# A transformer block on one Trainium2 core: an order written by a list scheduler, five-bank exp groups, and attention on four 32-wide strips

## The chip, the cores and the metric

The kernel runs on one core of a Trainium2 chip. The core's engines work side by side and meet only through semaphores: TensorE (PE) multiplies matrices and writes PSUM, VectorE (DVE) and ScalarE (ACT) compute element by element, GpSimd (POOL) does small things on SBUF, SyncE (SP) issues transfers. Each engine takes its instructions strictly in the order in which they stand in its program. The metric is the device time of one execution in microseconds (us). A profile of one further execution is at hand.

## The reference

One token sequence of 2048 rows of 640 passes through an adaLN-conditioned attention and a gated bilinear feed-forward; all tensors are bf16.

```python
mod = (_silu(c) @ w_mod)                      # six vectors of 640: sa, ca, ga, sb, cb, gb
h = _layernorm(x) * (1 + ca) + sa
q, k, v = split(h @ wqkv)                     # 32 heads of 20
p = softmax(q @ k.T * 20 ** -0.5)             # 2048 x 2048 for each head
x = x + ga * ((p @ v) @ wo)
h = _layernorm(x) * (1 + cb) + sb
x = x + gb * (((h @ w_gate) * (h @ w_up)) @ w_down)    # 640 -> 1536 -> 640
```

## The kernel before

**Layout.** Queries go in four chunks of 512; for each chunk and each group of heads the scores are computed transposed, with 128 keys on the partitions and 512 queries along the row. A *block* is one such 128x512 score tile of one head: 32 heads x 16 key tiles x 4 chunks = 2048 blocks. K and Q lie in tiles of four heads, each head padded to 32 rows (`KT_sb`, `QT_sb`), so that a score matmul has 32 rows and up to four of them can stand on different row strips of the array. V has 24 columns a head, the first of them 1, so that the row sums of the softmax fall out of the same matmul.

**A step.** Heads are taken in sets of three (`SETS`, eleven sets, the last with two). A step is one set and one key tile: three score matmuls (L1130) into one of two triples of PSUM banks, one exp by ACT over the triple (L1146, 128x1536 into a ring `Pbuf` of four), three PV matmuls (L1159) that accumulate into bank 6 on three column strips. There are 4 x 11 x 16 = 704 steps. After the 16 steps of a set, DVE transposes the result (L1183), takes the reciprocal of the row sums (L1187), multiplies (L1189) and transposes back (L1193) into `Oc`, in which each set has a row block of its own.

**What sets the order.** The order is a loop over steps: exp of step g, scores of step g+2, PV of step g, then `xs.inject(g)`. That call puts other matmuls, *X work*, into the gap, a bounded number of nanoseconds for each step, from a list of tasks whose accumulations all go to bank 7: first the projections that were not done before the loop, then, once a chunk of attention is finished, its *suffix*: out-projection (L959, eleven matmuls a round, one for each set), residual add (L968), LayerNorm (L980 to L988), the multiply and add with the modulation vectors (L990, L992), transposes (L999) and their eviction (L1005), gate (L1036), its eviction (L1041), up (L1049), the product (L1054), down (L1073), the last add (L1083), the store. w_down is scaled by the vector gb on DVE in every chunk (L934). A step with nothing to put in gets a filler matmul of 32 rows (L852). The suffix of the fourth chunk comes after the last exp, with all eight banks.

**The head.** Before the loop: POOL clears the padded weight tiles (L512 to L515) and then issues the load of wqkv (L561); ACT takes square roots (L583) and the sigmoid (L653); PE makes all six modulation vectors, broadcast over the partitions (L663); ACT copies the weights into padded tiles (L690 to L698); each of the four token tiles is normalised (L568 to L592), transposed (L615), evicted by ACT with shift and scale (L620), and gets the first half of V (L746, L752) and the first K and Q tiles (L724, L734). ACT then zeroes two row blocks of `Oc` (L861, L868).

## Time and profile before

| | us |
|---|---|
| time, median of three runs (lowest to highest) | 1135.11 (1135.11 to 1136.35) |
| span of the profiled execution, first to last instruction | 1138.6 |
| busy: PE, ACT, DVE, POOL | 952.1, 969.7, 390.4, 37.8 |
| first exp starts, last exp starts | 91.4, 1059.8 |
| mean granted PE clock | 0.913 |

The profiled execution has no time of its own beside its span; the span lies 3.5 us above the median of the runs. A row of a group in the profile reads: line, engine, operation, out<-in with shapes, count, then the busy time of the group and the mean duration of one in ns, then the idle time of the engine ahead of it and who ended it. A row of the order of time reads: start, length, engine, line, and in brackets the idle time before it. A row of windows reads: the window, its length, busy us of each engine with instruction counts, the granted clock as a share of full speed, the share of the DMA engines and GB/s.

### The profile page before, as it was taken

To read this page: it belongs to the slowest core of one execution; us is meant where nothing else is said; L and a number is where in the kernel's file an instruction comes from. 1 tells how busy PE (TensorE), PEld (TensorE's weight loads), DVE (VectorE), ACT (ScalarE), POOL (GpSimd) and SP (SyncE) were. 2 spreads that over 40 slices of the span, in tenths; PEclk is the share of its full clock that TensorE was granted. 3 is DMA by queue.
4 is the path that set the end of the run, shared out by engine and by line. 5 is a ranking of instruction groups with operands and counts; after the bars stand their busy time and mean duration, and the time that the engine had idled before them with its cause. 6 is when DMAs were issued, how large, how long until landed. Compare 5 with 4: busy or idle time off the path is not lost.

```text
span 1138.6 us, 14720 instructions
## 1 busy us (share of the span) xinstructions
PE 952.1 (84%) x6035; PEld 293.7 (26%) x6095; DVE 390.4 (34%) x690; ACT 969.7 (85%) x752; POOL 37.8 (3%) x52
## 2 busy tenths in 40 slices
PE   1677898899998888888997898889987888889778
PEld 0331222222222222222322222223222222223434
DVE  2741322344323333332114333321123333322475
ACT  1559999999999899999999999999987999999200
POOL 7000000000000000000000000000000000000000
PEclk9788999999989889898989779999977899989889
DMA  8100001000022001100230011100400011100422
GB/s 295 57 1 1 1 1 30 1 1 1 1 75 53 1 12 45 37 13 6 68 78 1 1 30 41 35 1 18 133 1 1 12 36 35 24 6 20 126 64 64
DMA packets 80418, 40.59 MB, mean 36 GB/s; under 512 B 64544, under 2 KB 80032, under 8 KB 80352
## 3 DMA queue, kind: packets, MB, share of 16 engines
q1 hardware_dynamic: 77328, 32.29, 11.0%
q10 hardware_dynamic: 2624, 4.92, 1.2%
q0 software_dynamic: 400, 2.46, 0.6%
q8 instruction: 48, 0.79, 0.3%
q14 instruction: 18, 0.15, 0.0%
HBM read 37.03 MB, written 2.62 MB: 35 GB/s over the span
## 4 chain that ended last, share of the span: by engine, by line
PE 39%; ACT 29%; issue 16%; DVE 13%; POOL 2%; another core or an unknown queue 0%; ACTq 0%; POOLq 0%
ACT Pbuf L1146 26%; PE ps_all L1159 9%; PE ps_all L1130 9%; PE ps_all L724 7%; PE ps_all L959 3%; PE ps_all L1036 3%; PE ps_all L1073 3%; PE ps_all L1049 2%; PE ps_all L746 2%; DVE OT L1183 2%; DVE KT_sb L734 1%; DVE QT_sb L734 1%; ACT hT L620 1%; PE ps_all L852 1%; DVE xn L990 1%
## 5 line engine op out<-in xcount | busy, mean ns | idle before, releaser
L1146 ACT ACTIVATE Pbuf<-ps_all 128x1536 bf16<-128x1536 f32 (+1 forms) x704 | 928.9, 1526 | 40.6 <-PE ps_all L1130 39.4
L1130 PE MATMUL ps_all<-QT_sb,KT_sb 32*128 32x512 bf16 x2048 | 296.1, 412 | 73.1 <-ACT Pbuf L1146 49.5
L1159 PE MATMUL ps_all<-Pbuf,V_sb 128*24 128x512 bf16 x2048 | 294.1, 412 | 9.0 <-DVE OT L1183 8.8
L1130 PEld LDWEIGHTS ps_all<-QT_sb,KT_sb 32*128 32x128 bf16 x2048 | 68.9, 92 | 323.7 <-ACT Pbuf L1146 244.2
L1159 PEld LDWEIGHTS ps_all<-Pbuf,V_sb 128*24 128x24 bf16 x2048 | 67.2, 89 | 189.4 <-issue 169.0
L959 PE MATMUL ps_all<-wo_sb,Oc 128*128 128x320 bf16 x352 | 76.7, 344 | 13.9 <-DVE h2T L1005 11.7
L1036 PE MATMUL ps_all<-h2T,wgst 128*128 128x512 bf16 x216 | 71.9, 410 | 9.8 <-DVE hprod L1054 4.4
L1073 PE MATMUL ps_all<-wd_sb,hprod 128*128 128x320 bf16 x384 | 72.5, 313 | 6.2 <-DVE wd_sb L934 5.4
L1049 PE MATMUL ps_all<-h2T,wust 128*128 128x512 bf16 x228 | 71.8, 398 | 4.9 <-DVE gsb L1041 3.4
L1183 DVE STREAM_TRANSPOSE OT<-ps_all 96x512 f32<-96x512 f32 (+1 forms) x44 | 31.3, 711 | 118.3 <-PE ps_all L1159 118.3
L1041 DVE COPY gsb<-ps_all 128x512 f32<-128x512 f32 x48 | 32.9, 685 | 89.8 <-PE ps_all L1036 82.4
L1054 DVE TENSOR_TENSOR hprod<-ps_all,gsb 128x512 bf16<-128x512 f32 x48 | 32.8, 684 | 89.9 <-PE ps_all L1049 78.8
L968 DVE TENSOR_TENSOR xck<-ps_all,xck 128x320 bf16<-128x320 f32 x32 | 15.3, 486 | 121.5 <-PE ps_all L959 121.5
L746 PE MATMUL ps_all<-Wv,hT 128*128 128x384 bf16 x160 | 40.6, 394 | 12.9 <-ACT hT L620 12.9
L1083 DVE TENSOR_TENSOR xck<-ps_all,xck 128x320 bf16<-128x320 f32 x32 | 15.5, 484 | 98.5 <-PE ps_all L1073 98.5
L724 PE MATMUL ps_all<-hT,Wk 128*128 128x512 bf16 x147 | 43.5, 394 | 6.3 <-DVE KT_sb L734 2.9
L724 PE MATMUL ps_all<-hT,Wq 128*128 128x512 bf16 x149 | 42.8, 383 | 5.3 <-issue 1.0
L734 DVE CAST KT_sb<-ps_all 128x512 bf16<-128x512 f32 x32 | 22.1, 691 | 67.1 <-PE ps_all L724 67.1
L959 PEld LDWEIGHTS ps_all<-wo_sb,Oc 128*128 128x128 bf16 x352 | 29.2, 106 | 51.8 <-issue 22.7
L734 DVE CAST QT_sb<-ps_all 128x512 bf16<-128x512 f32 x32 | 22.1, 692 | 56.0 <-PE ps_all L724 53.9
L1073 PEld LDWEIGHTS ps_all<-wd_sb,hprod 128*128 128x128 bf16 x384 | 30.3, 99 | 38.4 <-issue 17.9
L934 DVE TENSOR_TENSOR wd_sb<-wd_sb,mods_b 128x640 bf16<-128x640 bf16 x48 | 39.0, 813 | 0.0
(68 smaller groups left out, 433.5 us busy)
## 6 DMA issues: line engine op xcount, KB each, us to landing
wd_sb<-in_B_w_down_dram SPq DMA_DIRECT2D x4, 1920.0 KB, 9.4
wgst<-in_B_w_gate_dram SPq DMA_DIRECT2D x48, 160.0 KB, 2.7
wust<-in_B_w_up_dram SPq DMA_DIRECT2D x48, 160.0 KB, 2.8
wmod_sb<-in_w_mod_dram ACTq DMA_DIRECT2D x4, 1200.0 KB, 13.9
x<-in_A_x_dram SPq DMA_DIRECT2D x4, 640.0 KB, 7.1
xck<-in_A_x_dram SPq DMA_DIRECT2D x4, 640.0 KB, 4.3
out_dram<-xck SPq DMA_DIRECT2D x16, 160.0 KB, 1.8
wraw<-in_A_wqkv_dram POOLq DMA_DIRECT2D x5, 480.0 KB, 5.9
```

The lines of the kernel that those rows point to most:

```text
L724: fn = lambda e, b, kt=kt: e.matmul(psbank(b), Wx[:, kt, sg, :], hT[:, tc, kt, :], start=(kt == 0), stop=(kt == KT - 1))
L734: eve = dve.ins(lambda e: e.tensor_copy(dst[:, sg, tc * 512:(tc + 1) * 512], psbank(b)), inc=c_ev, waits=w)
L746: fn = lambda e, b, kt=kt: e.matmul(psbank(b)[:, 0:ncol], hT[:, tc, kt, (t % 4) * 128:(t % 4 + 1) * 128], Wv[:, kt, cc * ncol:(cc + 1) * n ...
L934: ev_wdp_l[0] = dve.ins(lambda e: e.tensor_tensor(wd_sb[:, fc, :], wd_sb[:, fc, :], mods_b[:, 2, :], ALU.mult), inc=c_ev, waits=[ev_wdl])
L959: fn = lambda e, b, j=j, tl=tl, nch=nch: e.matmul(ps_all[:, b, 0:320], Ocq[:, j, tl * 128:(tl + 1) * 128], wo_sb[:, j, nch * 320:(nch + 1) ...
L1036: fn = lambda e, b, kt=kt, stg=stg: e.matmul(psbank(b), wgst[:, stg, kt, :], h2T[:, kt, :], start=(kt == 0), stop=(kt == KT - 1))
L1049: fn = lambda e, b, kt=kt, stg=stg: e.matmul(psbank(b), wust[:, stg, kt, :], h2T[:, kt, :], start=(kt == 0), stop=(kt == KT - 1))
L1073: fn = lambda e, b, fc=fc, tl=tl, nch=nch: e.matmul(ps_all[:, b, 0:320], hprod[:, fc, tl * 128:(tl + 1) * 128], wd_sb[:, fc, nch * 320:(nc ...
L1130: fn = lambda e, bs=bs, i=i, sg=sg, s=s, cq=cq, kt=kt: e.matmul(ps_all[:, bs * 3 + i, :], KT_sb[32 * s:32 * s + 32, sg, kt * 128:(kt + 1) ...
L1146: fn = lambda e, sl=sl, nh=nh, bs=bs: e.activation(Pbuf[:, sl, 0:nh * 512], ps_sflat[bs][:, 0:nh * 512], ACT.Exp, scale=SCALE)
L1159: fn = lambda e, i=i, h=h, sl=sl, kt=kt: e.matmul(ps_all[32 * i:32 * i + VW, BO, :], V_sb[:, kt, h * VW:(h + 1) * VW], Pbuf[:, sl, i * 512 ...
L1183: ev_t1 = dve.ins(lambda e, rows=rows: e.transpose(OT[0:rows, :], ps_all[0:rows, BO, :]), inc=c_at, waits=[ev_pv[g], st["onorm"]] + extra)
```

## The change

The file is written anew. Arithmetic and results are the same, apart from where scalings are applied. What it does:

**The order comes from a list scheduler.** Every instruction is a task with a duration from a small table (for PSUM reads by DVE `ps_cost`, for SBUF `sb_cost`, 216 ns for a 512-column matmul, ACT `n/1.2 + 52`), dependencies, a priority and, for X work, a gate. A simulated clock advances while the kernel is being built; whenever an engine of the model is free it takes the ready task with the best priority, and the sequence that results is the program. PE takes, in this order: the next score group if its banks are free; PV if at least six blocks wait (or a ring runs low, or the set ends); X work; a filler. A filler is now a full 128-row matmul on 512 columns (L1475), put in whenever the modelled activity of the last 3.4 us is under a bound; there are 240, where there were 83. The gate of X work is a number of exp groups, spread evenly over the chunk that follows.

**Groups.** Heads are taken in eight sets of four, and the blocks of all sets follow each other in one list, which is cut alternately into groups of three (banks 0 to 2, ring `PA`) and of two (banks 3 and 4, ring `PB`): 410 exps of 1536 and 409 of 1024 columns (L944). X work gets banks 5 and 6, PV bank 7 on four column strips. V has 21 columns a head without padding; a PV matmul takes 32 columns, of which the last eleven belong to the next head and are not used.

**Head.** `x` and two of the six modulation vectors are loaded first; those two are computed as columns (25 one-column matmuls each, L626), the rest later. The rsqrt goes to POOL. Scores of item 0 (the first set) start when the first token tile is projected; the other three tiles follow while exps run.

**Ends of sets.** The four DVE steps stay (L1050 to L1058), on 128 rows. The second transpose writes `OcT`, from which 36 small SBUF-to-SBUF transfers per chunk put the heads into rows without gaps (L1069), so that an out-projection round has five matmuls (L1119), not eleven.

**Suffix.** The modulation is folded into the eviction after the transposes (L1156). POOL scales wo and w_down once (L858, L863). After the last exp the evictions of the gate are ACT's (L1199), and the gate and up weights of nine of the twelve column tiles are by then in the space of used-up queries. The code also holds a path that makes exps on DVE from shifted copies; `QUADS` is zero, so no such instruction is built.

In the rows below, `hT` is the normalised input transposed, `Wk`/`Wq`/`Wv` the projection weights, `KT`/`QT` the projected K and Q, `scol` the vector silu(c), `wm` parts of w_mod.

The start of PE's program before, up to the first scores (L1130):

```order
L663 MATMUL ps_all<-wmod_sb_84,SC_68 128x320 x60
L615 MATMUL ps_all<-ident_49,xn_10_58 128x128 x20
L746 MATMUL ps_all<-Wv_56,hT_54 128x384 x20
L724 MATMUL ps_all<-hT_54,Wk_55 128x512 x5
L724 MATMUL ps_all<-hT_54,Wq_90 128x512 x5
L615 MATMUL ps_all<-ident_49,xn_10_58 128x128 x20
L746 MATMUL ps_all<-Wv_56,hT_54 128x384 x20
L724 MATMUL ps_all<-hT_54,Wk_55 128x512 x5
```

(two more tiles follow in the same way), and now:

```order
L626 MATMUL ps_all<-scol_55,wm_20_68 128x1 x25
L626 MATMUL ps_all<-scol_55,wm_21_69 128x1 x25
L689 MATMUL ps_all<-ident_49,xn_87 128x128 x20
L738 MATMUL ps_all<-hT_88,Wk_89 128x512 x5
L738 MATMUL ps_all<-hT_88,Wq_90 128x512 x5
L770 MATMUL ps_all<-wV_91,hT_88 128x320 x5
L919 MATMUL ps_all<-QT_70,KT_67 128x512 x5
L770 MATMUL ps_all<-wV_91,hT_88 128x320 x10
L919 MATMUL ps_all<-QT_70,KT_67 128x512 x3
```

The first scores (L919) stand behind one token tile, not four. On ACT, what stands ahead of the first exp (L944) is now:

```order
L577 ACTIVATE ex_52<-csb_51 128x5
L718 COPY Wq_90<-wkq_82 128x5x4x20
L722 COPY Wq_90<-wkq_82 128x28x20 x5
L718 COPY Wk_89<-wkq_82 128x5x4x20
L722 COPY Wk_89<-wkq_82 128x28x20 x2
L696 ACTIVATE hT_88<-ps_all,mcol_56 128x512
L722 COPY Wk_89<-wkq_82 128x28x20 x2
L696 ACTIVATE hT_88<-ps_all,mcol_56 128x512
L722 COPY Wk_89<-wkq_82 128x28x20
L944 ACTIVATE PA_78<-ps_all 128x1536
```

Two of the five hT evictions of the first tile wait behind weight copies there. In the middle of the stream, during gate and up work, PE's program before is

```order
L1130 MATMUL ps_all<-QT_sb_86,KT_sb_85 128x512 x3
L1159 MATMUL ps_all<-Pbuf_78,V_sb_88 24x512 x3
L1049 MATMUL ps_all<-h2T_75,wust_94 128x512 x2
L1130 MATMUL ps_all<-QT_sb_86,KT_sb_85 128x512 x3
L1159 MATMUL ps_all<-Pbuf_78,V_sb_88 24x512 x3
L1049 MATMUL ps_all<-h2T_75,wust_94 128x512
```

and now

```order
L919 MATMUL ps_all<-QT_71,KT_67 128x512 x3
L1307 MATMUL ps_all<-PA_78,Vf_77 32x512 x3
L1307 MATMUL ps_all<-PB_79,Vf_77 21x512
L1307 MATMUL ps_all<-PB_79,Vf_77 32x512
L1307 MATMUL ps_all<-PA_78,Vf_77 32x512 x2
L1307 MATMUL ps_all<-PA_78,Vf_77 21x512
L919 MATMUL ps_all<-QT_71,KT_67 128x512 x2
L1191 MATMUL ps_all<-h2T_94,stg_97 128x512 x3
L919 MATMUL ps_all<-QT_71,KT_67 128x512 x5
```

PV stands in batches of seven or eight blocks behind every third score group, and X work in between. After the last exp PE had

```order
L959 MATMUL ps_all<-wo_sb_89,Oc_35_83 128x320 x44
L999 MATMUL ps_all<-ident_49,xn_22_70 128x128 x5
L959 MATMUL ps_all<-wo_sb_89,Oc_35_83 128x320 x22
L999 MATMUL ps_all<-ident_49,xn_22_70 128x128 x5
L959 MATMUL ps_all<-wo_sb_89,Oc_35_83 128x320 x22
L999 MATMUL ps_all<-ident_49,xn_22_70 128x128 x10
L1036 MATMUL ps_all<-h2T_75,wgst_93 128x512 x5
```

and now has

```order
L1475 MATMUL ps_all<-KT_67,ident_49 128x512 x12
L1119 MATMUL ps_all<-wo_98,Ocp_86 128x320 x40
L1475 MATMUL ps_all<-KT_67,ident_49 128x512 x6
L1151 MATMUL ps_all<-ident_49,xn_48_96 128x128 x20
L1475 MATMUL ps_all<-KT_67,ident_49 128x512
L1191 MATMUL ps_all<-h2T_94,stx_103 128x512 x10
```

All 40 out-projection matmuls stand together, and the transposes come after the fourth tile's LayerNorm. The diff, cut to the places that matter:

```diff
-    for g in range(min(lead, NSTEP)):
-        issue_scores(g)
-    for g in range(NSTEP):
-        P.cur_step = g
-        issue_exp(g)
-        if g + lead < NSTEP:
-            issue_scores(g + lead)
-        issue_pv(g)
-        ...
-        xs.inject(g)
...
-    SETS = [tuple(range(i, min(i + 3, H))) for i in range(0, H, 3)]
...
+SEM = 60.0
+PE_DRAIN = 170.0
+PE_SWITCH = 100.0
+ACT_LAT = 190.0
+DVE_LAT = 40.0
+DMA_RATE = 260.0
+HAM_W = 3413.3
+HAM_MIN = 2550.0
...
+CHUNKS = [(0, 512), (512, 512), (1024, 512), (1536, 512)]
+QUADS = [0, 0, 0, 0]
+def ps_cost(n):
+    return n * 1.042 + 110.0
+def sb_cost(n, rate):
+    return n * rate + 62.0
...
+    load_x(0, "sp", 1)
+    load_wm(0, wm_a[0], "act", 0)
+    load_wm(1, wm_a[1], "act", 1)
+    d_wK = load_w(1, "sp", 2, wkq[:, :, D:2 * D])
+    d_wQ = load_w(0, "act", 2, wkq[:, :, 0:D])
+    d_wV = load_w(2, "act", 3, wV[:, :, :])
+    load_x(1, "sp", 3)
+    load_x(2, "sp", 4)
+    load_x(3, "sp", 5)
...
+    GA = [0, 1, 2]
+    GB = [3, 4]
+    G = Slots([5, 6], "G")
+    BPV = 7
...
+    while ubuf:
+        k = 3 if gi_ % 2 == 0 else 2
+        glist.append(ubuf[:k])
+        ubuf = ubuf[k:]
+        gi_ += 1
...
+        ta = Task("act", nu * 512 / 1.2 + 52.0, fexp, [ts], prio=g, name=f"E{g}")
+        ta.acq = [(pool_, "p", nu)]
...
+        mc = VW if (4 * u.j + s) % 16 == 15 else 32
+        ...
+            ems.append(lambda e, i=i, kt=kt, stt=stt, stp=stp: e.matmul(
+                ps[32 * s:32 * s + mc, BPV, 0:u.n],
+                Vf[:, (kt * H + 4 * u.j + s) * VW:(kt * H + 4 * u.j + s) * VW + mc],
+                srcf()[:, i * u.n:(i + 1) * u.n], tile_position=(0, 32 * s), start=stt, stop=stp,
+                skip_group_check=True))
...
+    def pick_pe(t):
+        sc.pull("pe")
+        if pvstate["sidx"] < NG:
+            ts, us = score_q[pvstate["sidx"]]
+            if acquire_ready(ts, t):
+                start = mode_start("S", t)
+                dur, used = issue_S(ts, us, t, start)
+        ...
+        cands = pv_candidates(t, 10)
+        it = st_pv["item"]
+        if cands:
+            info = item_info[it]
+            nwork = sum(1 if k == "a" else 4 for k, _ in cands)
+            ring_low = min(len(pA.free), len(pB.free)) < RINGLOW
+            ending = info["left"] <= len(cands) or len(info["aq"]) < PVMIN
+            if nwork >= PVMIN or ring_low or ending:
+                pv_issue(cands, t)
+                return True
+        ...
+        rl = sc.readyl["pe"]
+        rl.sort(key=lambda x: (x.prio, x.seq))
+        ...
+        if pvstate["sidx"] > 0 and fill_ok(t):
+            start = mode_start("X", t)
+            task = Task("pe", 216.0, ffill, fill_deps, ctr="pex", mode="X", name="fill", acq=[(G, "g", 1)])
+            ...
+            task.emits = [lambda e: e.matmul(bank(b_), ident[:], KT[:, 0, 0:512])]
+            sc.activity(start, 512.0)
...
+        return sc.recent(t) < FILL_MIN
...
+        def gate(w):
+            g = gb + 9 + int((gl - 9) * 0.985 * rc_[1] / w_tot)
+            rc_[0] += 1
+            rc_[1] += w
+            return 0 if tail else g
...
+        t4 = dve(sb_cost(n, .55), lambda e: e.transpose(OcT[:, cell["s"], 0:n], OTn[:, 0:n]), [t3], prio=1.5)
...
+                return e.dma_start(Ocp[r0:r0 + nr, slot, b5, 0:n],
+                                   OcT[32 * s + 1 + ro:32 * s + 1 + ro + nr, cell["s"], 0:n])
...
+                        if tail:
+                            fa = lambda e: e.copy(gsb[:, gs, 0:n], ps[:, r.b["b"], 0:n])
+                            return [act(n / 1.2 + 60, fa, ds, prio=1e6)]
+                        return [dve(ps_cost(n), f, ds, prio=1)]
```

## Prediction

> **What bounds the kernel now.** I read the page's busy shares first, then the span cut into three windows, then the exp line on ScalarE, then the order of time at both ends.

> ```profile
> PE 952.1 (84%) x6035; PEld 293.7 (26%) x6095; DVE 390.4 (34%) x690; ACT 969.7 (85%) x752; POOL 37.8 (3%) x52
> 0.00:91.40 91.40, 44.10 (x248) 25.08 (x251) 43.49 (x108) 40.78 (x48) 25.17 (x20) 0.86 0.31 110
> 91.40:1061.20 969.80, 849.38 (x5465) 236.26 (x5519) 298.42 (x498) 928.91 (x704) 9.51 (x24) 0.92 0.10 27
> 1061.20:1138.60 77.40, 58.66 (x324) 32.37 (x325) 48.52 (x84) 0.00 (x0) 3.17 (x8) 0.89 0.26 57
> L1146 ACT ACTIVATE Pbuf<-ps_all x704: 1017/1519/1969, 91.4 to 1059.8; 128x1536 bf16<-128x1536 f32 x160, 128x1024 bf16<-128x1024 f32 x16
> ```

> The columns of a window are its length, the busy time of PE, PEld, DVE, ACT and POOL, then the granted clock. The middle window runs from the first exp to the end of the last, and ACT is busy 928.9 of its 969.8 us. Ahead of it lie 91.4 us without an exp, behind it 77.4 us with none left. So the time is a head, an ACT stream and a tail, and I price the three.

> The stream's own floor comes from two unbroken runs:

> ```profile
> 260.93 40.57 ACT L1146 ACTIVATE Pbuf<-ps_all 128x1536 bf16<-128x1536 f32 x30
> 1055.24 5.68 ACT L1146 ACTIVATE Pbuf<-ps_all 128x1024 bf16<-128x1024 f32 x6
> ```

> Neighbours overlap, so the pitch counts, not the duration. Thirty of the wide form take 40.57 us; less one duration (the maximum, 1.969) that is 38.6 over 29, 1.331 us each. The last six start between 1055.24 and 1059.8: 4.56 over 5, 0.91 us. The floor of the old stream is 640 x 1.331 + 64 x 0.91 = 910 us, and 969.8 - 910 = 60 us are stalls. One kind of place where they arise:

> ```profile
> 300.49 0.39 PE L1130 MATMUL ps_all<-QT_sb,KT_sb 32*128 32x512 bf16 x3
> 300.81 0.39 PE L1159 MATMUL ps_all<-Pbuf,V_sb 128*24 128x512 bf16 x3
> 301.13 0.61 PE L724 MATMUL ps_all<-hT,Wq 128*128 128x512 bf16 x2
> 301.67 0.39 PE L1130 MATMUL ps_all<-QT_sb,KT_sb 32*128 32x512 bf16 x3
> 846.47 0.61 PE L1130 MATMUL ps_all<-QT_sb,KT_sb 32*128 32x512 bf16 x3
> 847.01 0.61 PE L1159 MATMUL ps_all<-Pbuf,V_sb 128*24 128x512 bf16 x3
> 847.55 0.98 PE L959 MATMUL ps_all<-wo_sb,Oc 128*128 128x320 bf16 x3
> 848.46 0.61 PE L1130 MATMUL ps_all<-QT_sb,KT_sb 32*128 32x512 bf16 x3
> 849.12 1.45 ACT L1146 ACTIVATE Pbuf<-ps_all 128x1536 bf16<-128x1536 f32 x1 [0.54 <-PE ps_all L1130]
> 850.00:900.00 50.00, 40.91 (x264) 11.55 (x263) 18.32 (x35) 43.74 (x33) 2.37 (x6) 0.77 0.00 1
> ```

> At 300 us a score section costs 0.32, a PV section 0.32, two projection matmuls 0.54: with 0.216 per 512 columns, each section pays about 0.1 us for the switch. At 846 us the same sections cost 0.54, 0.53 and 0.91: a step takes 1.99 us, and ACT waits 0.54 for it. This is the half clock, which the last row shows as 0.77 over 50 us. It comes although PE is recorded busy for 40.9 of the 50.

> [...]

> **The change, part by part.**

> *Head.* Now: POOL clears buffers first and ACT's first real work waits for them; all six modulation vectors are computed before LayerNorm is applied; all four token tiles are projected before the first exp.

> ```profile
> 11.20 0.49 DVE L568 BATCH_NORM_STATS2 st<-x 128x6 f32<-128x320 bf16 x1 [11.20 <-DMA x<-in_A_x_dram]
> 11.61 0.48 DVE L569 BATCH_NORM_STATS2 st<-x 128x6 f32<-128x320 bf16 x1
> 19.36 1.28 ACT L583 ACT_TABLE_LOAD   x1 [19.36 <-POOL mhalf L520]
> 23.58 10.78 PE L663 MATMUL ps_all<-wmod_sb,SC 128*128 128x320 bf16 x60 [23.58 <-DVE SC L655]
> 48.64 0.42 DVE L574 BATCH_NORM_AGGREGATE mv<-st 128x2 f32<-128x12 f32 x4
> 55.98 1.51 DVE L592 TENSOR_SCALAR xn<-x,mv,rs 128x640 bf16<-128x640 bf16 x4
> L734 DVE CAST KT_sb<-ps_all 128x512 bf16<-128x512 f32 x32 | 22.1, 691 | 67.1 <-PE ps_all L724 67.1
> L752 DVE CAST V_sb<-ps_all 128x368 bf16<-128x368 f32 x32 | 17.3, 541 | 48.4 <-PE ps_all L746 48.4
> L1005 DVE COPY h2T<-ps_all 128x640 bf16<-128x640 bf16 x16 | 7.8, 486 | 7.9 <-PE ps_all L999 7.9
> L690 ACT COPY Wk<-wraw 128x640 bf16<-128x640 bf16 x5 | 3.2, 724 | 7.8 <-DMA wraw<-in_A_wqkv_dram 7.8
> wmod_sb<-in_w_mod_dram ACTq DMA_DIRECT2D x4, 1200.0 KB, 13.9
> ```

> After, x still lands at about 11 us. Two vectors as columns replace the twelve rounds: 50 one-column matmuls, at most 0.18 each (10.78 over 60), 9 us beside bn_stats and normalisation. On ACT twelve weight copies (0.72 at most) and two hT evictions stand ahead of the first exp, from about 15 us (Wq is third on ACT's queue, as much data as the first two of the old loads, 13.9 at the median): about 24 us, then K, Q and their evictions; the first exp is near 28. But only a quarter of item 0 (16 of its 64 score blocks of 512) can run then. The other tiles come out of one DVE queue. Up to the last K block of item 0 the order gives DVE 32 bn_stats x 0.40 = 12.8, 4 aggregates x 0.42 = 1.7, 4 normalisations x 1.51 = 6.0, 18 hT evictions x 0.49 (L1005 is the nearest row) = 8.8, 6 K/Q x 0.69 = 4.1, 12 V x 0.54 = 6.5: 40 us, from 11 to 51 if it never waits. It waits for the ACT evictions, for POOL's rsqrt and for PE in each tile; I take 6 us, so 57. Bounds: 51, and 68 with 5 us lost in each of four tiles. By then ACT has done 48 blocks and 2000 of 2048 remain.

> *Stream.* Groups of three and two alternate in five banks: 410 wide and 409 narrow, not 640 and 64. The 2000 blocks are 400 x 1.331 + 400 x 0.91 = 896 us; the whole new floor, 918, is 8 us more than the old.

> [...]

> *PE under the stream.* In chunks 1 to 3 the order gives, per chunk, about 205 score sections x 0.32 = 66 us, 78 PV sections of some 6.5 blocks on four column strips (two waves x 0.216 + 0.1 = 0.53) = 41, 59 us of other matmuls (61 to 70 of them fillers) and about 140 switches into them = 14: 180 us under 229 us of ACT. In chunk 0 the projections make it 228, no spare at all. PV on a fourth strip is in no row: running beside the others it costs nothing more, alone one wave of 0.216 x 310 sections = 67 us, still inside the spare of three chunks. I take the first, since three strips at 300.81 cost one wave.

> A new wait: a wide group must be written within the narrow exp, 0.91 us. It needs 0.39 from its start (300.49), which leaves 0.52; with the hand-overs on both sides I call 0.3 us usable before ACT notices. PV sections (0.53) and four projection matmuls (0.96) in a row can overrun that; X work behind a late DVE eviction as well, for PE takes its queue in order and the next scores stand behind. For stalls I take 30 us: 12 in chunk 0, 6 in each other, most at item ends. Bounds: 5 (the spare absorbs all) and 70 (below).

> *DMA and POOL.* The heads now reach packed rows through 144 small SBUF copies on SP, behind weight loads; no row shows one. Between rows

> ```profile
> out_dram<-xck SPq DMA_DIRECT2D x16, 160.0 KB, 1.8
> csb<-in_c_dram SPq DMA_DIRECT2D x1, 1.2 KB, 5.0
> L934 DVE TENSOR_TENSOR wd_sb<-wd_sb,mods_b 128x640 bf16<-128x640 bf16 x48 | 39.0, 813 | 0.0
> ```

> I take 1.8 to land. Under the stream 229 us of chunk cover them; in the tail they are on the path. The 17 weight scalings moved to POOL have a chunk to hide in; at 0.81 (DVE's L934) or threefold they cost nothing.

> *Tail.*

> ```profile
> 1061.40 0.71 DVE L1183 STREAM_TRANSPOSE OT<-ps_all 64x512 f32<-64x512 f32 x1 [11.71 <-PE ps_all L1159]
> 1063.14 0.70 DVE L1193 STREAM_TRANSPOSE Oc<-OTn 64x512 bf16<-64x512 bf16 x1
> 1063.90 8.98 PE L959 MATMUL ps_all<-wo_sb,Oc 128*128 128x320 bf16 x44 [2.23 <-DVE Oc L1193]
> 1074.66 0.88 DVE L968 TENSOR_TENSOR xck<-ps_all,xck 128x320 bf16<-128x320 f32 x2
> 1090.10 0.82 DVE L992 TENSOR_TENSOR xn<-xn,mods_b 128x640 bf16<-128x640 bf16 x1
> 1092.86 1.91 PE L1036 MATMUL ps_all<-h2T,wgst 128*128 128x512 bf16 x4 [1.17 <-DVE h2T L1005]
> 1109.81 1.24 PE L1036 MATMUL ps_all<-h2T,wgst 128*128 128x512 bf16 x5
> 1110.88 1.24 PE L1049 MATMUL ps_all<-h2T,wust 128*128 128x512 bf16 x5
> 1122.66 13.21 PE ps_all L1073 x96
> ```

> Last PV 0.5; the four DVE steps 2.5 (1061.40 to 1063.90); the copies 3.6 (four issues of about 0.45, then 1.8); out-projection with 40 matmuls for 88, where DVE now sets the pace: 8 adds x 0.44, 8 bn_stats x 0.40, aggregates 0.4 and normalisations 1.5 are 8.6, with the first round and the rsqrt 10.5; five transposes evicted 2.9; 24 gate/up rounds at 1.07 (1109.81 to 1110.88) plus the last product 26.4; down 13.2; the last add and store 2.6. Sum 62 against 77.4. The two modulation passes (L990, L992) are folded into the eviction, the w_down scaling and the gate evictions leave DVE.

> *Sum.* 57.6 (57 and one score section) + 896 + 62 = 1016, + 30 stalls = 1046 by the span. The profiled execution's span is 1138.6 while its runs read 1135.1 (median), so I take off 3.5: **1042 us**.

> **Rivals.**

> *Stalls near zero*: PE is nowhere late. 1016 + 5 - 3.5 = 1018. For it: 49 us of PE spare per chunk. [...] Against: chunk 0 has none, and DVE steps run longer than the table in the code assumes (the second transpose, L1193, 0.70 us against 0.34). Chance 0.10.

> *The clock is no better than now.* A mean of 0.92 in the stream window is half rate for 16% of it. All at half rate, PE needs about 318 us per chunk (205 x 0.54, 78 x 0.96, 2 x 59, 14) and by the same working 410 in chunk 0, in all 448 more than ACT's floor; 16% of that is 72: 1016 + 72 - 3.5 = 1085. For it: the out-projection, dense full-array work, shrinks from 352 to 160 matmuls and what is left is spread thin. Against: 240 fillers of 128 rows, where there were 83 of 32 rows. Chance 0.19.

> *Slower.* The same mechanism further on: the evenly thinned work keeps the array under what the gate wants, and half rate holds for more than (1138.6 - 1016) / 448 = 27% of the stream. At 35%: 1016 + 157 - 3.5 = 1170. Against: the stream now stands at 16%, and only single stretches such as 850 to 900 (0.77, that is 46%) pass 27%. Chance 0.05.

> *The head is not bought*: if the DVE chain, the loads or the copies ahead of the first exp hold item 0 until about 110 us, nothing but the tail remains: 1042 + 53 = 1095. Against: only 40 us of DVE work stands there. Chance 0.04.

> **How the numbers follow.** Forecast 0.62, with a range of its own from 1022 to 1065 (head 51 to 68, stalls 15 to 45). With 0.10, 0.19, 0.05 and 0.04 for the rivals, 1014 to 1098 leaves out the slower case and the edges of the others, under two in ten. A change within 0.2% (about what runs of this kernel can tell from none) needs a sum near 1135, between two cases: 0.01. Slower: the third rival, 0.05. Faster: 0.94.

> **What would show it.** First exp near 28 us, then gaps on ACT until about 57 and none after; ACT pitches of 1.33 and 0.90; PE's granted clock in the stream above 0.95; last exp near 984, the tail 62. It is wrong if ACT idles on scores for more than 45 us after 60 us, if the clock there is under 0.92, or if gate/up starts later than 22 us after the last exp.

## The result and the profile after

The changed kernel takes 1052.1 us (median; 1048.9 to 1056.0) where the kernel before takes 1135.3: a ratio of 0.927, 95% interval 0.924 to 0.929. Measured once more beside the last experiments it was 1054.4 (ratio 0.927, 0.925 to 0.930). The forecast was 1042, with a range of 1014 to 1098.

The profiled execution took 1055.98 us, its span is 1054.2. First the busy line, then four windows (up to the first exp; the 64 blocks of item 0; the other items; the tail), with the columns of the prediction's windows, then the two exp lines:

```profile
PE 882.6 (84%) x6120; PEld 270.2 (26%) x6120; DVE 294.8 (28%) x551; ACT 946.1 (90%) x847; POOL 53.5 (5%) x69
0.00:30.40 30.40, 9.86 (x90) 5.22 (x90) 15.86 (x31) 9.47 (x16) 12.96 (x14) 1.00 0.91 302
30.40:75.30 44.90, 40.42 (x350) 18.25 (x349) 32.82 (x86) 29.73 (x27) 5.00 (x7) 0.96 0.12 38
75.30:986.60 911.30, 777.39 (x5386) 216.98 (x5383) 220.13 (x382) 899.87 (x794) 32.34 (x41) 0.98 0.12 28
986.60:1054.20 67.60, 54.89 (x298) 29.72 (x298) 25.97 (x53) 7.03 (x12) 3.20 (x8) 0.92 0.03 12
L944 ACT ACTIVATE PA<-ps_all 128x1536 bf16<-128x1536 f32 x410 | 659.7, 1609 | 28.8 <-PE ps_all L919 28.6
L944 ACT ACTIVATE PB<-ps_all 128x1024 bf16<-128x1024 f32 x409 | 485.5, 1187 | 3.0 <-PE ps_all L919 2.9
```

The span lost 84.4 us in three places. The first exp stands at 30.4 instead of 91.4 us: 61.0. From the first to the last exp it is 956.2 us instead of 969.8: 13.6, because stalls fell from 60 to 41 us while the floor rose from 910 to 915.4 (410 x 1.331 + 409 x 0.904). The tail is 67.6 instead of 77.4: 9.8. PE's clock in the stream is 0.98 where it was 0.92, and of the 31.8 us for which the two exp lines waited (5.3 of them ahead of the first exp), 31.5 ended on scores (L919).

Of the 41 us of stalls 16 lie in item 0 (44.9 us; the window holds 26 exps with 65 blocks, 29.1 at the floor) and 24.5 in the other 31 items (911.3 less 1984 blocks at the floor, 886.8; one of these blocks ran in the window of item 0 already, which makes 0.4 us, the same in every run with these groups). Item 0 is the head that runs under the first exps. These are VectorE and GpSimd ahead of the first exp, then the K casts, which release the scores of one token tile after the other, and the gaps on ScalarE that they leave (the number in brackets is the wait just before):

```profile
7.28 4.99 DVE L578 TENSOR_SCALAR ex<-ex 128x5 f32<-128x5 f32 x1 [5.89 <-ACT ex L577]
14.37 3.23 DVE L657 BATCH_NORM_STATS2 st<-x 128x6 f32<-128x320 bf16 x8
4.32 4.15 POOL L572 MEMSET Wk<- 128x4480 bf16 x1
8.41 3.83 POOL L573 MEMSET Wq<- 128x4480 bf16 x1
45.07 0.69 DVE L746 CAST KT<-ps_all 128x512 bf16<-128x512 f32 x1 [0.69 <-PE ps_all L738]
55.85 0.69 DVE L746 CAST KT<-ps_all 128x512 bf16<-128x512 f32 x1
66.39 0.69 DVE L746 CAST KT<-ps_all 128x512 bf16<-128x512 f32 x1 [0.94 <-PE ps_all L738]
46.68 1.45 ACT L944 ACTIVATE PA<-ps_all 128x1536 bf16<-128x1536 f32 x1 [9.38 <-PE ps_all L919]
57.03 1.45 ACT L944 ACTIVATE PA<-ps_all 128x1536 bf16<-128x1536 f32 x1 [3.47 <-PE ps_all L919]
67.57 1.02 ACT L944 ACTIVATE PB<-ps_all 128x1024 bf16<-128x1024 f32 x1 [2.31 <-PE ps_all L919]
```

The last K block of item 0 is cast at 66.4 us. One row stands out: five elements a partition took VectorE 4.99 us, and it ended when GpSimd's second memset ended (8.41 + 3.83 = 12.24 against 7.28 + 4.99 = 12.27).

The tail by TensorE's order of time, and its windows from the out-projection to the first gate/up matmuls:

```profile
993.83 7.28 PE L1119 MATMUL ps_all<-wo,Ocp 128*128 128x320 bf16 x40 [4.13 <-DMA Ocp<-OcT]
1006.58 2.31 PE L1151 MATMUL ps_all<-ident,xn 128*128 128x128 bf16 x20 [4.18 <-DVE xn L1141]
1009.64 20.80 PE L1191 MATMUL ps_all<-h2T,stx 128*128 128x512 bf16 x90 [0.31 <-DVE h2T L1156]
993.80:1001.00 7.20, 7.17 (x41) 4.69 (x42) 4.64 (x12) 0.00 (x0) 0.79 (x2) 0.76 0.01 2
1006.50:1009.60 3.10, 2.74 (x21) 2.16 (x21) 2.38 (x6) 0.00 (x0) 0.00 (x0) 0.50 0.00 0
1009.60:1013.00 3.40, 3.36 (x10) 1.27 (x11) 0.00 (x0) 0.59 (x1) 0.00 (x0) 0.63 0.00 0
```

The out-projection starts 7.2 us after the last exp, gate/up 23.0 us after it. Behind the wait of 4.13 us for the copies the clock is 0.76 in the out-projection, and 0.50 to 0.63 where the transposes and gate/up begin.

### The profile page after: what moved, and what is told of

Read it like the earlier page. It is cut to its first block, busy times and chain, and to the rows that moved or that the text cites. A ratio compares the mean times of both kernels' runs of the same rounds, so it can differ in the third digit from the quotient of the medians.

```text
span 1054.2 us, 14917 instructions
## 1 busy us (share of the span) xinstructions
PE 882.6 (84%) x6120; PEld 270.2 (26%) x6120; DVE 294.8 (28%) x551; ACT 946.1 (90%) x847; POOL 53.5 (5%) x69
## 4 chain that ended last, share of the span: by engine, by line
ACT 45%; PE 30%; issue 19%; DVE 5%; ACTq 1%; POOL 1%; SPq 0%; DMA 0%; POOLq 0%
ACT PB L944 25%; ACT PA L944 19%; PE ps_all L919 8%; PE ps_all L1307 6%; PE ps_all L738 5%; PE ps_all L1191 4%; PE ps_all L1221 2%; PE ps_all L770 2%; PE ps_all L1119 1%; PE ps_all L1475 1%; DVE st L657 1%; DVE xn L676 1%; DVE ex L578 0%; PE ps_all L1151 0%; DVE hT L699 0%
## 5 line engine op out<-in xcount | busy, mean ns | idle before, releaser
L944 ACT ACTIVATE PA<-ps_all 128x1536 bf16<-128x1536 f32 x410 | 659.7, 1609 | 28.8 <-PE ps_all L919 28.6
L944 ACT ACTIVATE PB<-ps_all 128x1024 bf16<-128x1024 f32 x409 | 485.5, 1187 | 3.0 <-PE ps_all L919 2.9
L919 PE MATMUL ps_all<-QT,KT 32*128 32x512 bf16 x2048 | 323.1, 391 | 131.8 <-ACT PA L944 91.9
L919 PEld LDWEIGHTS ps_all<-QT,KT 32*128 32x128 bf16 x2048 | 78.0, 91 | 428.2 <-ACT PA L944 240.5
L1307 PE MATMUL ps_all<-PA,Vf 128*32 128x512 bf16 (+1 forms) x1230 | 171.8, 392 | 0.6 <-ACT PA L944 0.6
L1307 PE MATMUL ps_all<-PB,Vf 128*32 128x512 bf16 (+1 forms) x818 | 170.2, 395 | 0.0
L1191 PE MATMUL ps_all<-h2T,stg 128*128 128x512 bf16 x390 | 119.9, 395 | 0.3 <-DVE h2T L1156 0.3
L1475 PE MATMUL ps_all<-KT,ident 128*128 128x512 bf16 x240 | 79.8, 394 | 0.0
L1221 PE MATMUL ps_all<-wd,hprod 128*128 128x320 bf16 x384 | 70.1, 305 | 0.8 <-DVE hprod L1206 0.8
L1050 DVE STREAM_TRANSPOSE OT<-ps_all 128x512 f32<-128x512 f32 x32 | 22.9, 716 | 120.7 <-PE ps_all L1307 120.7
L1199 ACT CAST gsb<-ps_all 128x512 bf16<-128x512 f32 x12 | 7.0, 586 | 42.9 <-PE ps_all L1191 42.9
L1307 PEld LDWEIGHTS ps_all<-PA,Vf 128*32 128x32 bf16 x1230 | 32.2, 94 | 37.8 <-issue 34.8
L750 DVE TENSOR_SCALAR QT<-ps_all 128x512 bf16<-128x512 f32 x32 | 22.1, 690 | 68.2 <-PE ps_all L738 68.2
```

Of the source, the lines that this page charges most:

```text
L750: f = lambda e, ci=ci, so=so, n=n: e.tensor_scalar(QT[ci][:, j, :], ps[:, r.b["b"], so:so + n], QSCALE, None, op0=ALU.mult)
L919: ems.append(lambda e, i=i, kt=kt: e.matmul(dstf()[:, i * u.n:(i + 1) * u.n], KT[32 * u.s:32 * u.s + 32, u.j, kt * 128:(kt + 1) * 128], QT ...
L944: return e.activation(pbuf[:, cellp["p"], 0:nu * 512], ps[:, b0:b0 + nu, :].rearrange("p b c -> p (b c)"), AFT.Exp, scale=ESCALE)
L1050: t1 = Task("dve", ps_cost(n), lambda e: e.transpose(OT[:, 0:n], ps[:, BPV, 0:n]), [], prio=0.0, name=f"T1.{it}")
L1191: f = lambda e, b, k=k, cell=wbuf[w_]: e.matmul(ps[:, b, 0:n], cell["t"][:, k, :], h2T[:, k, 0:n], start=(k == 0), stop=(k == KD - 1))
L1221: f = lambda e, b, fc=fc, tl=tl, hf=hf: e.matmul(ps[:, b, 0:320], hprod[:, fc, tl * 128:(tl + 1) * 128], wd_sb[:, fc, 320 * hf:320 * hf + ...
```

## The experiments

In all of them ratios and medians are against runs of the kernel before on the same chip (1135.4 to 1136.0 us). "Item 0" and "the other items" are the windows used above.

### What holds TensorE's clock

**Fillers taken out.** Only the 20 behind the last scores remain:

```diff
-        if pvstate["sidx"] > 0 and fill_ok(t):
+        if pvstate["sidx"] >= NG and fill_ok(t):
```

> The changed kernel with its 240 filler matmul groups cut to the 20 behind the last scores. The fillers' results are read by nobody, so nothing of the output is missing. My theory: the 128-row fillers hold the granted clock of TensorE at 0.98 in the stream. Without them each chunk of 229 us has some 45 us of matmuls less, the half rate comes back in at least 16% of the stream as in the kernel before (granted clock there 0.92 or less), scores come late, and the time rises from 1052 by 20 to 70 us, 40 in the middle: 1092. Rival: the order of the work, not the fillers, keeps TensorE from standing idle; then the clock stays above 0.96, the PE queue only gets shorter, and the time is 1045 to 1055.

1122.9 us, ratio 0.985 (0.979 to 0.992): 71 us slower than the changed kernel, just past the theory's upper end of 70. The same 50 us of stream, first of the changed kernel, then of this one, and below them this kernel's window of the other items:

```profile
600.00:650.00 50.00, 41.23 (x288) 10.39 (x287) 11.60 (x18) 50.00 (x46) 0.00 (x0) 1.00 0.16 37
600.00:650.00 50.00, 42.05 (x244) 9.31 (x244) 10.78 (x17) 46.58 (x42) 0.00 (x0) 0.80 0.15 34
74.00:1058.00 984.00, 856.67 (x5166) 213.49 (x5163) 217.54 (x382) 914.43 (x794) 31.69 (x41) 0.79 0.11 26
```

TensorE is recorded busier without the fillers (42.05 for 41.23), with 44 matmuls fewer, at a clock of 0.80 for 1.00. Busy time says nothing of the clock here. The stalls of the other items rise from 24.5 to 97.2 us; that is the whole loss. The 45 us of matmuls less per chunk, which I had expected, were too many: 220 fillers at 0.216 us are 48 us in all, 12 a chunk. But TensorE also has other gaps without fillers, so this alone doesn't tell idle time from work.

**The same fillers on a quarter of the rows.**

```diff
-            task.emits = [lambda e: e.matmul(bank(b_), ident[:], KT[:, 0, 0:512])]
+            task.emits = [lambda e: e.matmul(bank(b_), ident[0:32, :], KT[0:32, 0, 0:512], tile_position=(0, 0))]
```

> The changed kernel with its 240 fillers at the same places and of the same 512 columns, but on a quarter of the array's rows (32 instead of 128). TensorE's busy and idle times in the order are thus unchanged; only how much of the array works in a filler is smaller. Theory after the kernel without fillers (1122.9 us, granted clock 0.79 in the stream): the clock is granted by the work done in the array, so small fillers hardly hold it; clock 0.80 to 0.88 in the stream, time 1085 to 1123. Rival: the fillers help because they fill idle time; then the clock stays at 0.97 or more and the time at 1049 to 1056.

1118.1 us, ratio 0.984 (0.979 to 0.988). The fillers of the changed kernel, then of this one (busy us, mean ns; min/median/max ns where there are three), and this one's window of the other items:

```profile
L1475 PE MATMUL ps_all<-KT,ident x240: 379/389/634, 154.0 to 1008.7; 128*128 128x512 bf16 x120
L1475 PE MATMUL ps_all<-KT,ident x240: 374/384/630, 152.9 to 1065.6; 32*128 32x512 bf16 x120
74.20:1042.70 968.50, 836.09 (x5326) 217.18 (x5383) 220.50 (x382) 910.45 (x794) 32.26 (x41) 0.85 0.11 26
```

As many fillers, as long (0.384 and 0.389 us at the median), at the same places: only the rows differ, and the clock is 0.85 for 0.98. Of the 71 us that the fillers are worth, these keep 5 at most; the two ratios, 0.985 and 0.984, are the same within their intervals. TensorE's recorded idle time among the other items has not grown: 132.4 us here (968.5 less 836.1) and 127.3 without fillers, where the changed kernel has 133.9. Single gaps are short: the longest in the changed kernel's stream is 1.1 us, and without fillers the longest wait in its rows from 640 to 655 us is 0.95. So the clock here follows how much of the array works (0.98 at 128 rows, 0.85 at 32), and idle time doesn't explain it; filling gaps isn't enough.

**The kernel before with full fillers.**

```diff
-    xs.filler = lambda e: e.matmul(ps_all[:, BXW, :], KT_sb[0:32, 0, 0:128], QT_sb[0:32, 0, 0:512],
-                                   tile_position=(0, 0))
+    xs.filler = lambda e: e.matmul(ps_all[:, BXW, :], KT_sb[:, 0, 0:128], QT_sb[:, 0, 0:512])
```

> The kernel before, with its 83 filler matmuls made of 128 rows instead of 32; nothing else is changed. My theory: the clock is granted by how much of the array works in a window, not only by whether it stands idle, so the same number of fillers on the whole array raises the stream's granted clock from 0.92 to 0.94 or more and takes 8 to 25 us off 1135. Rival: only idle time counts; a filler of 128 rows lasts as long as one of 32, so clock and time stay (1131 to 1139).

1130.8 us, ratio 0.994 (0.992 to 0.997). Its stream:

```profile
89.70:1053.50 963.80, 846.80 (x5517) 235.61 (x5517) 298.42 (x498) 928.76 (x704) 9.47 (x24) 0.95 0.10 27
```

The clock rose from 0.92 to 0.95, as the theory had it, and the stream is 6.0 us shorter; the time fell by 5, less than the 8 that I set as the least. It also lies only just outside the rival's 1131 to 1139, so the clock speaks for the theory more than the time does. 83 full fillers bring half of the way from 0.92 to 0.98; how many the rest needs was not tried in this kernel.

**Without the even pacing.** Out-projection and feed-forward of a chunk start from the ninth exp group on:

```diff
-            g = gb + 9 + int((gl - 9) * 0.985 * rc_[1] / w_tot)
+            g = gb + 9
```

> The changed kernel without the spreading of the out-projection and feed-forward work of a chunk over the next chunk's exps: it may start from the ninth exp group on, as soon as TensorE has a gap; 356 fillers instead of 240 fill what that leaves. Theory: the fillers hold the clock (kernel without them 1122.9 us), so it stays at 0.97 or more without the spreading, and only the bursts of projection matmuls after a chunk's start make scores late: +2 to +8 us, 1054 to 1060. Rival: the even spreading is why the stream's stalls fell from 60 to 24.5 us; without it they come back to 45 or more: 1072 and above.

1059.4 us, ratio 0.935 (0.928 to 0.941). The other items:

```profile
73.80:990.20 916.40, 786.81 (x5417) 226.76 (x5499) 219.65 (x382) 904.20 (x794) 32.39 (x41) 0.96 0.12 28
```

The stalls are 29.6 us for 24.5, the clock 0.96, just under the 0.97 of the theory; the time is within it. Three of the four runs took 1057.4 to 1060.5 us, one 1073.1 at a mean clock of 0.924 for 0.96. So pacing is worth some 5 us, and the rival's 1072 and above did not come, here with 356 fillers.

### The head

**First exp held until all K stands.**

```diff
+            if g == 0:
+                deps += kt_ready[(0, 3)]
```

> The changed kernel, but the first exp waits until K of all four token tiles stands in place, as in the kernel before; the work ahead of it is the same. My theory: about half of what the head gained is that 64 score blocks (28.6 us of ScalarE at 1.331 and 0.904 us per group) run while tiles 1 to 3 are still prepared. First exp then near 66 us instead of 30, the last exp 17 to 20 us later, time 1070. Rival: the head gains only because its preparation is shorter, and item 0 is paced by the projections anyway (its stalls were 15.8 us): then item 0 runs without stalls afterwards and the time rises by 5 us at most, to 1057.

1072.2 us, ratio 0.943 (0.938 to 0.947), 18 to 20 us slower than the changed kernel. Its first exp, the preparation's window, and the window of all exps:

```profile
65.79 1.45 ACT L946 ACTIVATE PA<-ps_all 128x1536 bf16<-128x1536 f32 x1 [40.63 <-PE ps_all L919]
30.00:65.80 35.80, 26.91 (x202) 14.12 (x200) 30.51 (x82) 0.01 (x1) 3.81 (x6) 0.81 0.15 46
65.80:1000.80 935.00, 792.43 (x5539) 221.15 (x5538) 222.59 (x387) 927.63 (x819) 33.03 (x41) 0.99 0.12 28
```

The last exp ends 14.2 us later (1000.8 for 986.6): 35.4 us of later start, less item 0's stalls, 15.8, of which 0.3 are left, less 5.6 of stalls further on (18.9 for 24.5). In the runs' medians it is 18 to 20. So the overlap is worth some 14 to 20 us of the head's gain, and the shorter preparation the rest: even held, the first exp stands at 65.8 and not at 91.4. The theory is right in size. The K cast of the last tile came at 64.6 us here, with no score and no PV on TensorE ahead of it, so these are not what holds the tiles up. That the chain is that long by itself doesn't follow: the clock was 0.81 here, where it is 0.96 in item 0 of the changed kernel, and the V projections stand in between as before.

**GpSimd's memsets later.** Both large ones behind the first tile's hT:

```diff
-    p_wk2 = pool(2700, lambda e: e.memset(Wk[:, :, 1:NSET, :], 0.0), prio=3)
-    p_wq2 = pool(2700, lambda e: e.memset(Wq[:, :, 1:NSET, :], 0.0), prio=4)
...
+            pz2["K"] = pool(3900, lambda e: e.memset(Wk[:, :, 1:NSET, :], 0.0), [t_hT[0][-1]], prio=30)
+            pz2["Q"] = pool(3900, lambda e: e.memset(Wq[:, :, 1:NSET, :], 0.0), [t_hT[0][-1]], prio=31)
```

> The changed kernel with GpSimd's two large memsets (128x4480 each, for the padded weights of head sets 1 to 7) moved behind the first tile's transposes. In the profile of the changed kernel a 128x5 TENSOR_SCALAR on VectorE took 4.99 us and ended within 0.05 us of the second of these memsets. My theory: the memset held VectorE off; without it that row takes about 0.2 us, the first BATCH_NORM_STATS2 starts near 11 us instead of 14.4, the first exp comes 3 to 6 us earlier than 30.4, and the time falls by about 4 us to 1048. Rival: VectorE waited there for something else, a transfer or its own queue; the row stays near 5 us, and the time within 1 us of 1052. The memsets could disturb VectorE at the new place as well: then item 0 loses later what the first exp gains.

1057.1 us, ratio 0.929 (0.925 to 0.934): no gain. VectorE, and what became of ScalarE:

```profile
7.25 0.17 DVE L577 TENSOR_SCALAR ex<-ex 128x5 f32<-128x5 f32 x1 [5.86 <-ACT ex L576]
12.93 0.16 DVE L631 TENSOR_SCALAR mcol<-ps_all 128x5 f32<-128x5 f32 x1 [3.99 <-PE ps_all L625]
13.01 3.23 DVE L656 BATCH_NORM_STATS2 st<-x 128x6 f32<-128x320 bf16 x8
28.23 1.45 ACT L945 ACTIVATE PA<-ps_all 128x1536 bf16<-128x1536 f32 x1 [5.28 <-PE ps_all L920]
34.05 2.92 ACT L721 COPY Wk<-wkq 128x560 bf16<-128x560 bf16 x5
36.84 2.92 ACT L721 COPY Wq<-wkq 128x560 bf16<-128x560 bf16 x5
```

The row fell from 4.99 to 0.17 us: the memset held VectorE off, that is shown. But the step behind it waits until 12.93 for the modulation columns, so only 1.4 us reach bn_stats and 2.2 the first exp. And the weight copies that wait for the memsets now stand between the first exps, 5.6 us of ScalarE; item 0 ends at 77.6 instead of 75.3. A stall of 5 us in plain sight was worth 1.4, because the wait behind it ended only that much earlier.

**Less work on VectorE.** Two of five hT evictions of every tile on ScalarE:

```diff
-                if tc == 0 and k % 2 == 1:
+                if k % 2 == 1:
```

> The changed kernel with two of the five hT evictions of token tiles 1 to 3 on ScalarE, as those of tile 0 are (six instructions of 0.78 us there for 0.49 to 0.54 us on VectorE). In the changed kernel item 0 took 44.9 us for 28.6 us of exps; K casts stand at 27.1, 45.1, 55.9 and 66.4 us. Theory: VectorE's queue (busy 32.8 of those 44.9 us) paces the tiles; 2.9 us less of it bring the last K cast to 62 to 64 us, item 0's stall falls from 15.8 to 11 to 14 us, and the time to 1047 to 1050. Rival: each tile is paced by hand-overs between TensorE and VectorE and by the rsqrt on GpSimd, which stay: K cast at 65 or later, time within 1.5 us of 1052.

1059.3 us, ratio 0.931 (0.927 to 0.935). The last K cast, of this kernel:

```profile
66.91 0.69 DVE L746 CAST KT<-ps_all 128x512 bf16<-128x512 f32 x1 [1.89 <-PE ps_all L738]
63.84 1.06 ACT L944 ACTIVATE PB<-ps_all 128x1024 bf16<-128x1024 f32 x1
64.74 0.83 ACT L696 ACTIVATE hT<-ps_all,mcol 128x512 bf16<-128x512 bf16 x1
```

Not earlier than the 66.39 of the changed kernel: the theory fails, 2.9 us less work on VectorE don't shorten the chain. The rival has the K cast right, but not the time, which it put within 1.5 us of 1052. And hand-overs are not shown to be the cause: the last tile's second eviction now stands behind an exp on ScalarE (the last two rows), so the same chain may have lost there what it gained on VectorE.

**V behind the next tile's K.**

```diff
-            v_round(t, 0, 14 + 20 * tc)
+            v_round(t, 0, 35 + 20 * tc)
```

> The changed kernel with the V projections of a token tile put behind the next tile's transposes and K on TensorE (they stood ahead of them). With six hT evictions taken off VectorE, item 0 had not become shorter (last K cast at 66.9 us), so the amount of VectorE's work is not what paces the tiles. Theory: TensorE takes its queue in order, and the next tile's transposes stand behind 20 V matmuls whose two banks wait for VectorE's evictions; with V behind them the last K cast comes at 58 to 63 us, item 0's stall falls by 2 to 6 us and the time by as much, 1046 to 1050. Rival: the chain normalise, transpose, evict, project, cast with its hand-overs is that long by itself; the K casts keep their distance of 10.7 us, time within 1.5 us of the changed kernel's.

1057.6 us, ratio 0.930 (0.928 to 0.933), beside 0.927 (0.925 to 0.930) for the changed kernel: nothing gained. The last K cast and two exps of this kernel:

```profile
63.37 0.69 DVE L746 CAST KT<-ps_all 128x512 bf16<-128x512 f32 x1 [1.88 <-PE ps_all L738]
76.26 1.45 ACT L944 ACTIVATE PA<-ps_all 128x1536 bf16<-128x1536 f32 x1 [0.51 <-PE ps_all L1307]
82.73 1.45 ACT L944 ACTIVATE PA<-ps_all 128x1536 bf16<-128x1536 f32 x1 [1.74 <-PE ps_all L919]
```

The cast moved by 3 us, to the edge of what the theory said (58 to 63), but the exps didn't follow: item 0 still stalls for 14.6 us, and item 1 for 3.2 where it was 0.5. The V work is only put off, into item 1. What of the 10.7 us between K casts is the chain and what is TensorE's queue isn't settled by this.

### The groups, and a better version

**Three and three from the start.** Six score banks and one for projections:

```diff
-    GB = [3, 4]
-    G = Slots([5, 6], "G")
+    GB = [3, 4, 5]
+    G = Slots([6], "G")
...
-        k = 3 if gi_ % 2 == 0 else 2
+        k = 3
```

The second ring is widened to three blocks and the gates count exps of three blocks.

> The changed kernel with exp groups of three and three blocks in six score banks (683 exps instead of 819) and one bank left for projections instead of two. By the pitch of 1.331 us the stream's floor falls by 6.6 us. If nothing else mattered: 1045. Theory: with one bank each projection group waits for the eviction of the one before (0.7 us after 5 matmuls of 0.216), chunk 0, which had no spare on TensorE, and the head lose more than that: 1055 to 1075, most of it in the first 300 us. Rival: the spare of chunks 1 to 3 and the longer narrow window (1.33 for 0.91 us) outweigh it: 1042 to 1050.

1084.7 us, ratio 0.953 (0.949 to 0.957). Item 0 (21 groups, 63 of its 64 blocks) and the other items:

```profile
35.00:121.00 86.00, 62.89 (x359) 21.85 (x361) 30.98 (x74) 29.39 (x22) 9.33 (x9) 0.68 0.06 20
121.00:1019.70 898.70, 727.86 (x5219) 199.40 (x5304) 216.75 (x380) 891.30 (x662) 26.14 (x36) 0.97 0.12 29
```

More than the theory's 1055 to 1075, and in another place than I had it: all of the loss is in the head, 86 us for item 0 instead of 45, at a clock of 0.68; how much of that is the bank and how much the clock, this run doesn't tell. From item 1 on, chunk 0 included, one bank is enough, and the stalls are even fewer: 898.7 less 1985 blocks at 1.331 for three (880.7) is 18.

**Two banks for the first 52 groups, three and three from there.** In the core:

```diff
-        k = 3 if gi_ % 2 == 0 else 2
+        k = 3 if gi_ % 2 == 0 or gi_ >= NSW else 2
...
+            if pvstate["sidx"] == GW:
+                ok5 = False
+                for k5, (i5, rel5) in enumerate(G.free):
+                    if i5 == 5 and all(r.done + SEM <= t for r in rel5):
+                        ok5 = True
...
```

The gates of the projections and of the X work are set anew for the new number of exps.

> The changed kernel with groups of three and two blocks for the first 52 exps (two projection banks, as now) and of three and three from there on (one projection bank). The kernel with three and three from the start took 1084.7 us; its item 0 lasted 93 us for 45, and after that the items followed each other at the pitch of 1.331 us a group, without stalls. Theory: two projection banks are needed only while item 0 is prepared; from there the wider groups save (2048 - 130) blocks x (0.447 - 0.444) = 6 us at most of floor and some stalls: 1044 to 1049. Rival: chunk 0's projections after item 1 need the second bank in this order, and the gain goes into stalls there: 1051 to 1060.

1042.5 us, ratio 0.918 (0.915 to 0.920), 12 us faster than the changed kernel beside it, more than the theory's 5 to 10. Its windows:

```profile
30.40:75.20 44.80, 39.60 (x346) 18.21 (x349) 32.81 (x86) 29.69 (x26) 4.97 (x7) 0.96 0.12 38
75.20:972.20 897.00, 723.67 (x5229) 200.22 (x5311) 219.98 (x382) 890.79 (x667) 32.00 (x41) 0.98 0.12 29
972.20:1040.80 68.60, 55.33 (x293) 30.03 (x296) 26.09 (x53) 7.04 (x13) 3.20 (x8) 0.89 0.03 11
```

The other items take 897.0 for 911.3: 6 us of floor, as counted, and 8 of stalls. The 8 fit what a narrow exp costs: while it runs, 0.90 us, the next three blocks must be written; under a wide exp there are 1.33. That is argued, for the gates changed with the groups. (The expectation gives item 0 of the three-and-three kernel 93 us and its later items no stalls; by the windows above it was 86 us, with 18 us of stalls behind it.)

**The same, with V later and part of the last out-projection early.** Four of five products of six rounds (heads of earlier items) run while the last heads are normalised and copied:

```diff
+                if tail and 2 * tl + hf < 6:
+                    dk = [x for b5 in range(KD - 1) for x in oc_k[(ci, b5)]]
...
+                    r = Round(mms, dk + t_wo + [d_xc], after, pr(), gate=NG - 1, name=f"op{ci}.{tl}", late=oc_ready[ci])
```

> The same, with V behind the next tile's K, and with the first four of the five matmuls of six of the last out-projection's eight products done while the last heads are still being copied (four wait for nothing of the last item). Theory: the parts add up: 6 us of floor, 2 to 6 of item 0, and 2 us in the tail, because the out-projection at 993.8 us ran at half clock and VectorE waited 1.6 us for it: 1038 to 1046. Rival: after the copies VectorE's additions and statistics pace the tail, and item 0 does not move; then it stands where the kernel with only the banks changed stands, within 2 us.

1037.7 us, ratio 0.914 (0.911 to 0.916): the best of all, 1.6% under the changed kernel. TensorE after the last exp, which ends at 969.5:

```profile
969.88 2.89 PE L1141 MATMUL ps_all<-wo,Ocp 128*128 128x320 bf16 x20
976.76 4.02 PE L1141 MATMUL ps_all<-wo,Ocp 128*128 128x320 bf16 x16 [4.00 <-DMA Ocp<-OcT]
990.66 21.18 PE L1218 MATMUL ps_all<-h2T,stx 128*128 128x512 bf16 x88 [0.74 <-DVE h2T L1183]
```

Gate/up now starts 21.2 us after the last exp for 23.0 in the changed kernel, and the tail is 66.1 us for 68.6 in the kernel with the banks alone. That is the 2 us expected there. Item 0 and item 1 together are no shorter than without the V part (the stall only moves), so the parts don't all add up. The other 2.7 us of the difference stand in the items behind them (865.6 us for 868.3); no run takes them apart.

## Why the prediction was right, and where it was not

Its sum, taken to the end of item 0 (57.6 and 16 blocks more, 64.7), reads 64.7 + 889 + 30 + 62 = 1045.7 by the span. Measured: 75.3 + 886.8 + 24.5 + 67.6 = 1054.2. The sign and the mechanism held (a shorter head that runs under exps, fewer stalls at a better clock, a shorter tail), and the forecast was 10 us short: head and tail were sized 16 us too small together, stalls and floor 8 us too large, so the errors cancelled in part.

- **Head: 10.6 us too small.** First exp near 28: it was 30.4. DVE's 40 us of work were to end at 57 with 6 us of waiting; they began 3.4 us later than the 11 I set and ended at 67.1, with 38.8 us of work and 13.9 of waiting. The waiting was the mis-sized part, and what it waits for is not isolated. The sum of VectorE's work is not it alone (less of it: last K cast at 66.9), nor are scores and PV on TensorE (none ahead of it: 64.6, at a lower clock); V's place in TensorE's order is worth 3 us of the cast (63.4) and nothing of the time. Hand-overs between the engines fit what is left; so does TensorE's own queue, busy for 40.4 of item 0's 44.9 us. The upper bound of 68, 5 us lost in each tile, was the better guess. The stall under the memset was not foreseen, and cost 1.4 us of it.
- **Gaps until about 57 and none after**: they lasted until 67.6.
- **Floor**: the pitches of 1.33 and 0.90 came as said, the sum within 2 us.
- **Stalls: 30 expected, 24.5 measured.** The split was wrong: chunk 0, where I had put 12 for want of spare on TensorE, has 4 after item 0. PV in four column strips at no cost, which no row had shown, stands: eight blocks take 0.55 us to the next section (61.67 less 61.12), where I had 0.53 for six and a half.

```profile
61.12 0.40 PE L1307 MATMUL ps_all<-PA,Vf 128*32 128x512 bf16 x3
61.13 0.60 PE L1307 MATMUL ps_all<-PB,Vf 128*32 128x512 bf16 x2
61.35 0.39 PE L1307 MATMUL ps_all<-PA,Vf 128*32 128x512 bf16 x3
61.67 0.23 PE L689 MATMUL ps_all<-ident,xn 128*128 128x128 bf16 x1
```

- **Clock above 0.95**: 0.98. The reason given, 240 fillers of 128 rows for 83 of 32, was an estimate before the result and is the reason shown: 0.98 with fillers of 128 rows, 0.85 with 32, 0.79 without. What the slower rival calls the gate is known here by this granted clock alone. The rivals built on the clock priced the half rate too high: 448 us for a stream wholly at half rate. (The clock records of the traces before and after hold only full and half rate, 1.0 and 0.5, so I read a mean of 0.85 as 30% at half.) With the quarter-row fillers the stream was at half rate for 30% of it (0.85), 26 points more than the changed kernel, and its stalls grew by 57 us, not by 116; without fillers for 42% (0.79), 38 points, and they grew by 73, not by 170. Even so the time was 1122.9: the rival of 1170, set at 35%, was priced about twice too high.
- **Tail: 62 expected, 67.6 measured.** Copies 4.3 for 3.6; from the out-projection to gate/up 15.8 for 13.4; gate/up 28.0 for 26.4; the end 3.3 for 2.6. Part of it is the clock (0.76 in the out-projection, 0.50 to 0.63 around the start of gate/up): I had priced the wait for the copies, and the matmuls behind it at full rate. That the wait brings the half rate is not shown: no run takes it away. The mark "gate/up not later than 22 us after the last exp" was missed by one: by its own sign this term was wrong.
- **From span to median**: 3.5 us off expected, 2.1 measured, by luck. It is no fixed offset: in the later runs of the kernel before, each execution's span lies about 2 us under its own time (1133.4 for 1135.5), so the profiled execution with its span of 1138.6 was only a longer one than the median, and the same holds for the profile after (1055.98 for a median of 1052.1).

Idle time alone doesn't explain the half rate in this kernel: with TensorE's idle time the same (132.4 and 133.9 us), rows alone moved the clock from 0.98 to 0.85, and in the changed kernel's own stream the half rate came (551.3 to 558.1 us, for one) without any gap of TensorE longer than 1.1 us.

## What to carry to other kernels

Where small matmul tiles leave most of the array empty, fill gaps with work on all 128 rows (here 0.98 of the clock, with 32 rows 0.85) and judge by the granted clock, never by TensorE's busy share (here 42.05 us of 50 at a clock of 0.80, 41.23 at 1.00). Don't take the sum of one engine's work for the length of a chain of tiles: here 39 us of work on VectorE were spread over 53, and moving some of it to ScalarE did not shorten the chain. When a shared resource is short in one stage only (here PSUM banks for projections in item 0), change the split when that stage ends: it brought 12 us here.
